# Linear attention followed by a gated long convolution on one core: another order of the same 1477 steps

## The chip, the cores and the metric

The kernel runs on one core of a Trainium2 chip. A core has five engines that run side by side, each with a queue of its own that it works off strictly in order: TensorE (PE, matrix products, with weight loads shown apart as PEld), VectorE (DVE), ScalarE (ACT), GpSimd (POOL) and SyncE (SP), which here only issues DMAs. Engines wait for each other by semaphores. Matrix products are written to PSUM, eight banks of 128 x 2 KB, which DVE and ACT read out to SBUF; POOL works on SBUF alone. The metric is the device time of one execution in microseconds, the median of several runs.

## What is computed

```python
def phi(x):                                   # feature map, 64 -> 2 * 128
    proj = np.einsum('bhsd,df->bhsf', x, w_phi)
    proj = proj - np.max(np.abs(proj), axis=-1, keepdims=True)
    return np.concatenate([np.exp(proj), np.exp(-proj)], axis=-1)
q_p, k_p = (phi(q), phi(k))                   # 8 batches, 8 heads, 576 rows
kv = np.einsum('bhsf,bhsd->bhfd', k_p, v)
z = np.sum(k_p, axis=2)
num = np.einsum('bhsf,bhfd->bhsd', q_p, kv)
den = np.einsum('bhsf,bhf->bhs', q_p, z)[..., None] + 1e-06
x = (num / den)                               # -> (8, 576, 512), heads side by side
...
proj = x @ w_proj                             # (512, 1536): x1, x2, x3
X2 = np.fft.rfft(x2, n=S, axis=1)
H = np.fft.rfft(filter_fft, n=S, axis=0)[None, :, :]
x2_conv = np.fft.irfft(X2 * H, n=S, axis=1)
y = x1 * x2_conv * x3
return (y @ w_out).astype(np.float32)
```

The Fourier transforms over 576 rows are done as matrix products with tables of cosines and sines that the kernel makes itself at the start.

## The kernel before

The whole kernel is a list of words, `PLAN`. The last function, `run`, goes through it and calls one method for each word, so that the list fixes the order on every engine, and with it each engine's queue:

```python
for word in PLAN.split():
    name, _, bank = word.partition("@")
    self.bank = int(bank) if bank else None
    f, *args = name.split(",")
    getattr(self, f)(*[int(a) if a.isdigit() else a for a in args])
```

`X1e,DVE,2,0@6` is the method `X1e` with engine DVE, batch 2, block 0 and PSUM bank 6. Words of one batch are mixed with words of the batches before and after it. Where two words stand next to each other on different engines, the list does not say which runs first; only the order among words of the same engine, and the data, do. All words of one batch `b`, in the order of the data:

- `load` (and `loadh`, half a batch) brings q, k or v in on POOL's DMA queue, in rings of two buffers each; `trh` transposes q and k by DMA on SP's queue. For batch 0, `pt` transposes on PE and `pte` copies out of PSUM.
- `Qn`, `Qnt`, `Pk`, `Pkt` (L638, L646, L631): products with `w_phi` in which the rows lie on the partitions. `maxq`, `maxk`, `maxqt`, `maxkt` (DVE, L707) take the largest absolute value. `ex,k`, `exkt` (ACT, L693, L696) take the exponentials of k, `m` and `p` for the two signs.
- `mhi` (ACT), `mlo`, `trm` (PE), `trme`: the maxima of q, transposed. `Pq`, `Pqt` (L665, L671): q's products the other way round, with the maxima subtracted. `ex,q`, `exqt` (ACT): their exponentials.
- `em` (ACT) and `vs` (L749): v times the exponential of k's maxima, with POOL or DVE. `KV` (L764) sums over the rows, `KVe` copies it out.
- `NE`, `NEt` (L778, L787): the numerator and denominator. `rc`, `rct` and `xn`, `xnt` (DVE, L797, L809) divide.
- `trx`, `trxt` (SP, L816, L821) transpose the result by DMA into `xT`, `xTt`; `ptx`, `ptxe` do it on PE for three quarters of batch 0. `f1` (L846) and `f2` (L852) are folds, sums and differences in SBUF, with POOL or DVE.
- `F` (L858, L862): the transform of the folded rows. `Fe` copies it out, `Xl` repeats a few columns of it. `X2` (L897): the product with the middle third of `w_proj`; `Y1` (DVE, L902, L907): times the filter's spectrum; `m3` (L911): a sum in SBUF, with POOL or DVE.
- `X1`, `X3` (L919) and `X1t`, `X3t` (L928): the other two thirds of `w_proj` with `xT`; `X1e`, `X1te` copy, `tm`, `tmt` (DVE, L960, L964) multiply.
- `I` (L972), `Ie` (ACT), `Ip`, `Im` (DVE, L993), `ym` (L1038), or `J` (L1028) and `yj` (DVE, L1032): back from the spectrum, times x1 x3. `yt` moves the last rows of two batches together.
- `O` (L1049): the product with `w_out`; `Oe` copies it into `o`, a ring of four buffers; `st` (L1058) stores a half of it, on SP's queue or at the very end on ACT's.

At the start there are also the tables (`cols_*`, `gi_*`, `ang`, `frac`, `sin`, `gen_*`), the filter (`fl_load`, `ft`, `fa`, `fb`, `rev`, `Ff`, `Ffe`, `H`, `He`, `Hl`), and `wz`, two products of zeros that have no result and keep PE busy. `w_load` brings the weights in. `copy` gives a copy to ACT if the word says ACT, and to DVE otherwise, so `ft,POOL` runs on DVE (L297).

Of the kernel before, what the change touches and what calls it, by code (L numbers as in the profile page):

```python
# [37 lines left out]
pt,k,0,0,1@3 sin,0 maxq,0,0@4 Pk,0,0@0 pte,ACT,k,0,0,1@3 pt,k,0,1,1@6 fa,POOL,1 pt,k,0,1,0@7
maxk,0,0@0 pte,ACT,k,0,1,1@6 Qn,0,2@4 pte,ACT,k,0,1,0@7 pte,DVE,q,0,1,1@2 maxq,0,2@4 Pk,0,1@6
Qn,0,3@2 ft,POOL fa,POOL,0 maxq,0,3@2 ex,k,m,0,0@0 wz,9@4 Qnt,0@4 ex,k,p,0,0@0 maxqt,0@4 Pk,0,2@2  # L40
maxk,0,2@2 ex,k,m,0,1@6 Pk,0,3@4 w_load,proj,1 rev@0 ex,k,p,0,1@6 maxk,0,3@4 mhi,0 ex,k,p,0,2@2
maxk,0,1@6 ex,k,m,0,2@2 one Pkt,0@6 mlo,DVE,0 ex,k,m,0,3@4 trm,0@2 wz,1@3 maxkt,0@6 trh,q,1,0
fb,0@0 trme,ACT,0@2 wz,12@3 em,m,0,0 ex,k,p,0,3@4 vs,POOL,m,0,0 Pq,0,1@2 trh,q,1,1 fb,1@0 em,p,0,0
exkt,m,0@6 Pq,0,2@4 exkt,p,0@6 ex,q,m,0,1@2 wz,25@0 trh,k,1,0 vs,POOL,p,0,0 ex,q,p,0,1@2 Qn,1,0@0
wz,14@6 trh,k,1,1 em,m,0,1 ex,q,p,0,2@4 maxq,1,0@0 Pq,0,3@2 w_load,proj,2 KV,0,0@6 ex,q,m,0,2@4
vs,DVE,m,0,1 em,p,0,1 ex,q,p,0,3@2 Ff,1@4 vs,POOL,p,0,1 KVe,DVE,0,0@6 Pk,1,1@0 ex,q,m,0,3@2
Ffe,DVE,1@4 Qn,1,3@6 ex,k,m,1,1@0 maxq,1,3@6 NE,0,1@4 Ff,0@2 w_load,proj,0 maxk,1,1@0 KV,0,1@6
Ffe,ACT,0@2 load,v,1 rc,0,1@4 ex,k,p,1,1@0 gen_ends,POOL Pq,0,0@2 xn,0,1@4 KVe,DVE,0,1@6 Qnt,1@4
trx,0,1 ex,q,m,0,0@2 Pk,1,0@0 maxqt,1@4 Ff,2@6 load,k,2 ex,q,p,0,0@2 maxk,1,0@0 NE,0,3@4 load,q,2
# [12 lines left out]
KVe,ACT,1,0@6 load,q,3 late Y1,0,2@5 ex,k,p,2,1@2 trm,1@6 vs,POOL,p,1,1 X2,0,0@7 ex,k,m,2,0@0
trme,DVE,1@6 Y1,0,1@4 X2,0,4@5 ex,k,m,2,1@2 Pq,1,1@0 Y1,0,4@5 load,v,3 X2,0,3@4 ex,q,m,1,1@0
Y1,0,0@7 w_load,out Pkt,2@2 ex,q,p,1,1@0 X1,0,1@5 maxkt,2@2 load,k,3 Y1,0,3@4 X3,0,2@7 exkt,m,2@2
m3,POOL,0,0 exkt,p,2@2 Qn,2,1@0 X1e,ACT,0,1@5 tm,0,2@7 Pq,1,0@2 Pq,1,2@4 maxq,2,1@0 ex,q,m,1,0@2
X1t,0@7 X3t,0@6 ex,q,p,1,0@2 m3,DVE,0,1 X3,0,1@0 X1te,DVE,0@7 em,m,2,0 ex,q,p,1,2@4 tmt,0@6
NE,1,0@2 vs,POOL,m,2,0 tm,0,1@0 J,0,0@6 ex,q,m,1,2@4 rc,1,0@2 xn,1,0@2 NE,1,1@0 trx,1,0 yj,0,0@6
# [6 lines left out]
NEt,1@6 maxq,2,3@2 O,0,1@1 trh,k,3,0 f2,POOL,1,0,0 rct,1@6 O,0,2@0 xnt,1,0@6 Oe,ACT,0,1@1 xnt,1,1@6
maxqt,2@4 Pk,2,3@2 trh,k,3,1 Oe,ACT,0,2@0 F,1,2@6 maxk,2,3@2 F,1,3@4 Fe,ACT,1,2@6 F,1,0@0 trh,q,3,0
Fe,ACT,1,3@4 X1,1,3@6 Fe,DVE,1,0@0 ex,k,m,2,3@2 Qn,2,2@4 st,SP,0,1,0 X1e,DVE,1,3@6 em,m,2,1 F,1,1@0
vs,POOL,m,2,1 trxt,1 maxq,2,2@4 X1,1,2@7 Fe,ACT,1,1@0 Qn,3,2@0 st,SP,0,1,1 mhi,2 X2,1,2@4
X1e,ACT,1,2@7 maxq,3,2@0 ex,k,p,2,3@2 load,q,4 X3,1,2@5 Y1,1,2@4 mlo,POOL,2 load,q,5 trm,2@2
X2,1,1@3 trme,ACT,2@2 em,p,2,1 tm,1,2@5 vs,POOL,p,2,1 Pq,2,0@1 Y1,1,1@3 Qn,3,0@4 Pq,2,1@6
ex,q,m,2,0@1 X3,1,3@0 maxq,3,0@4 ex,q,p,2,0@1 load,k,4 X1,1,0@3 ex,q,p,2,1@6 tm,1,3@0 Pq,2,2@4  # L80
ex,q,m,2,1@6 Pkt,3@0 X2,1,3@2 maxkt,3@0 X2,1,0@6 exkt,m,3@0 Y1,1,3@2 exkt,p,3@0 X1,1,1@7
ex,q,m,2,2@4 Y1,1,0@6 NE,2,1@0 X1e,ACT,1,1@7 X3,1,0@2 X1e,ACT,1,0@3 rc,2,1@0 m3,POOL,1,0 xn,2,1@0
ex,q,p,2,2@4 NE,2,0@6 tm,1,0@2 X1t,1@3 rc,2,0@6 Pqt,2@4 xn,2,0@6 X1te,ACT,1@3 Pq,2,3@0 exqt,p,2@4
Xl,DVE,1 Pk,3,1@2 f1,POOL,2,0,1 KV,2,1@6 trh,q,4,1 exqt,m,2@4 maxk,3,1@2 ex,q,p,2,3@0 f1,POOL,2,0,0
X2,1,4@4 st,SP,0,0,0 KVe,ACT,2,1@6 ex,q,m,2,3@0 trx,2,0 NE,2,2@6 m3,POOL,1,1 Y1,1,4@4 X3t,1@5
ex,k,p,3,1@2 rc,2,2@6 NEt,2@0 xn,2,2@6 trx,2,1 X3,1,1@4 ex,k,m,3,1@2 tmt,1@5 rct,2@0 f2,POOL,2,0,0
xnt,2,0@0 NE,2,3@6 trx,2,2 xnt,2,1@0 I,1,0@2 rc,2,3@6 f2,POOL,2,0,1 xn,2,3@6 Ie,1,0@2 I,1,1@0
Im,1,0@2 trx,2,3 Ie,1,1@0 J,1,2@6 tm,1,1@4 f1,POOL,2,1,0 Ip,1,1@0 Im,1,1@0 trxt,2 Pk,3,2@4 Ip,1,0@2
Pk,3,0@0 yj,1,2@6 ex,k,p,3,2@4 ym,POOL,1,0 J,1,3@2 st,SP,0,3,0 maxk,3,0@0 ex,k,m,3,2@4 st,SP,0,3,1
X1,2,0@6 ym,POOL,1,1 st,SP,0,0,1 yj,1,3@2 ex,k,p,3,0@0 X3,2,0@7 trh,k,4,1 maxk,3,2@4 load,v,4  # L90
em,m,3,0 ex,k,m,3,0@0 O,1,0@2 X1e,DVE,2,0@6 trh,q,4,0 em,p,3,0 F,2,0@4 f1,DVE,2,1,1 X1,2,2@6
# [1023 lines left out]
```

## Time and profile before

| | us |
|---|---|
| three runs | 306.68, 306.43, 314.14 |
| median | 306.68 |
| profiled execution, span from the first to the last instruction | 311.6 |
| busy: PE, DVE, ACT, POOL | 281.0, 268.6, 216.3, 203.8 |
| mean granted clock of PE in that span | 0.974 |

The profiled execution's time beyond its span is not shown. In the rows of the profile a group is named by its line in the code, the engine, the operation and the tiles; "idle before" is the time in which that engine stood still just before, with what ended it.

### The profile page before, as it was taken

To read this page: it belongs to the slowest core of one execution; us is meant where nothing else is said; L and a number is where in the kernel's file an instruction comes from. 1 tells how busy PE (TensorE), PEld (TensorE's weight loads), DVE (VectorE), ACT (ScalarE), POOL (GpSimd) and SP (SyncE) were. 2 spreads that over 40 slices of the span, in tenths; PEclk is the share of its full clock that TensorE was granted. 3 is DMA by queue.
4 is the path that set the end of the run, shared out by engine and by line. 5 is a ranking of instruction groups with operands and counts; after the bars stand their busy time and mean duration, and the time that the engine had idled before them with its cause. 6 is when DMAs were issued, how large, how long until landed. Compare 5 with 4: busy or idle time off the path is not lost.

```text
span 311.6 us, 10240 instructions
## 1 busy us (share of the span) xinstructions
PE 281.0 (90%) x4331; PEld 205.3 (66%) x4360; DVE 268.6 (86%) x447; ACT 216.3 (69%) x345; POOL 203.8 (65%) x163
## 2 busy tenths in 40 slices
PE   1968977999999996999899799999999999999992
...
GB/s 162 235 203 159 136 202 193 105 190 133 91 164 204 94 110 170 116 160 107 114 198 82 131 160 153 172 175 160 84 117 4 56 93 69 19 110 21 1 115 192
DMA packets 72735, 40.20 MB, mean 129 GB/s; under 512 B 53040, under 2 KB 67504, under 8 KB 72688
## 3 DMA queue, kind: packets, MB, share of 16 engines
...
q8 instruction: 34, 0.56, 0.8%
...
## 4 chain that ended last, share of the span: by engine, by line
PE 70%; DVE 12%; DMA 7%; ACT 5%; issue 3%; SPq 1%; POOL 0%; DVEq 0%; POOLq 0%
PE ps L919 16%; PE ps L897 10%; PE ps L1049 8%; PE ps L764 5%; PE ps L972 4%; PE ps L778 4%; DMA xT<-xn 4%; DMA out_dram<-o 3%; PE ps L1028 3%; PE ps L858 3%; PE ps L862 3%; PE ps L928 2%; DVE mq L707 2%; PE ps L665 2%; PE ps L638 2%
## 5 line engine op out<-in xcount | busy, mean ns | idle before, releaser
L919 PE MATMUL ps<-xT,wproj 128*128 128x256 bf16 x512 | 65.8, 275 | 4.3 <-DVE x1s L960 2.3
L919 PEld LDWEIGHTS <-wproj 128*128 128x128 bf16 x512 | 48.6, 98 | 14.5 <-issue 5.1
L707 DVE TENSOR_REDUCE mk<-ps 128x8 f32<-128x1024 f32 (+1 forms) x40 | 44.0, 1110 | 5.9 <-ACT HTo L295 2.2
L707 DVE TENSOR_REDUCE mq<-ps 128x8 f32<-128x1024 f32 (+1 forms) x40 | 44.0, 1110 | 5.5 <-PE ps L638 4.5
L749 POOL TENSOR_TENSOR vm<-vn,vm 128x1152 bf16<-128x1152 bf16 x14 | 30.4, 2178 | 18.2 <-ACT vm L743 18.2
L749 POOL TENSOR_TENSOR vp<-vn,vp 128x1152 bf16<-128x1152 bf16 x16 | 34.8, 2180 | 10.5 <-ACT vp L743 10.3
L911 POOL TENSOR_TENSOR T<-T,T 128x1024 bf16<-128x1024 bf16 x12 | 25.5, 2124 | 21.9 <-DVE T L907 21.8
L693 ACT ACTIVATE Ekp<-ps 128x1024 bf16<-128x1024 f32 x32 | 32.8, 1030 | 6.6 <-DVE mk L707 3.3
L1038 POOL TENSOR_TENSOR yT<-cv,x1s 128x576 bf16<-128x576 f32 x19 | 24.3, 1289 | 18.3 <-DVE x1s L964 12.8
L852 POOL TENSOR_TENSOR xf<-SD 128x512 bf16<-128x512 bf16 x27 | 31.2, 1170 | 6.7 <-DVE SD L846 5.3
L693 ACT ACTIVATE Ekm<-ps 128x1024 bf16<-128x1024 f32 x32 | 32.8, 1033 | 3.6 <-DVE mk L707 2.7
L693 ACT ACTIVATE Eqm<-ps 128x1024 bf16<-128x1024 f32 x32 | 32.9, 1034 | 3.1 <-PE ps L671 2.9
L1049 PE MATMUL ps<-wout,yT 128*128 128x512 bf16 x133 | 34.3, 385 | 0.7 <-issue 0.2
L693 ACT ACTIVATE Eqp<-ps 128x1024 bf16<-128x1024 f32 x32 | 32.5, 1031 | 3.4 <-PE ps L671 3.3
L846 POOL TENSOR_TENSOR SD<-xn 128x512 bf16<-128x512 bf16 x23 | 26.5, 1160 | 12.6 <-DVE xn L797 12.6
L897 PE MATMUL ps<-wproj,XF 128*128 128x512 bf16 x117 | 30.3, 380 | 0.7 <-issue 0.2
L295 ACT CAST x1s<-ps 128x512 bf16<-128x512 f32 (+1 forms) x30 | 16.0, 548 | 13.1 <-PE ps L928 8.4
L797 DVE TENSOR_TENSOR xn<-ps,r 128x512 bf16<-128x512 f32 x32 | 22.0, 689 | 1.1
L1049 PEld LDWEIGHTS <-yT 128*128 128x128 bf16 x144 | 13.4, 99 | 14.1 <-issue 0.6
L990 ACT COPY es<-ps 128x288 f32<-128x288 f32 x21 | 8.5, 404 | 20.3 <-PE ps L972 19.8
L960 DVE TENSOR_TENSOR x1s<-ps,x1s 128x512 bf16<-128x512 f32 x32 | 21.7, 683 | 0.6 <-ACT x1s L295 0.4
L778 PE MATMUL ps<-KVs,Eqp 128*128 128x65 bf16 x256 | 19.6, 192 | 2.2 <-DVE mq L707 0.6
...
## 6 DMA issues: line engine op xcount, KB each, us to landing
...
```

Of the source, the lines that this page charges most:

```text
L693: self.nc.scalar.activation(e, p, AF.Exp, bias=0.0, scale=1.0 if g == "p" else -1.0)
L707: self.nc.vector.tensor_reduce(out=out, in_=src, axis=AX.X, op=ALU.max, apply_absolute_value=True)
L749: self.eng(eng).tensor_tensor(out=t[:, :, :, 0:64], in0=self.at("vn", b)[:, 2 * X:2 * X + 2], in1=t[:, :, :, 64:65].to_broadcast([128, 2, ...
L778: self.mm(self.pb(u, 65 * a, 65 * a + 65), E, KVs[:, u, v, s, :], start=(s == 0), stop=(s == 1))
L797: self.nc.vector.tensor_tensor(out=o, in0=n[:, :, :, 0:64], in1=self.at("r", 4 * b + v).to_broadcast([128, 2, 4, 64]), op=ALU.mult)
L846: self.eng(eng).tensor_tensor(out=o[:, :, 2 * i:2 * i + 2, :], in0=x[:, :, 0:2, :], in1=x[:, :, 2:4, :], op=ALU.subtract if i else ALU.add)
L852: self.eng(eng).tensor_tensor(out=o[:, :, 2 * i:2 * i + 2, :], in0=x[:, :, 0:4:2, :], in1=x[:, :, 1:4:2, :], op=ALU.subtract if i else ALU ...
L897: self.mm(self.pb(0), l, w[:, kt, 512:1024], start=(kt == 0), stop=(kt == 3))
L911: self.eng(eng).tensor_tensor(out=Y, in0=Y, in1=self.at(f"T{2 * e + 1}", b), op=ALU.add)
L919: self.mm(o[:, d], w[:, kt, f0 + 128 * m:f0 + 128 * m + 128], y[:, 1, ::-1, ::-1] if d else y[:, 0], start=(kt == 0), stop=(kt == 3))
L1038: self.eng(eng).tensor_tensor(out=self.at("yT", b)[:, m, 0:SEQ], in0=self.turn_of("cv", (b, m)).rearrange("p x h t -> p (x h t)"), in1=sel ...
L1049: self.mm(self.pb(0), y[:, kt, 128 * c:128 * c + 128], w[:, kt, :], start=(kt == 0), stop=(kt == 3))
```

## The change

Only the list is changed. It has 1477 words before and after, and the same work in them; the order is another on every engine, many words have another PSUM bank, and 88 words have another engine. Counted over the words whose engine differs (before to after, on the engine named):

| word | DVE before | DVE after | the other engine |
|---|---|---|---|
| `f1` | 7 | 5 | POOL 5, 7 |
| `f2` | 4 | 4 | POOL 4, 4 |
| `m3` | 2 | 1 | POOL 1, 2 |
| `vs` | 2 | 1 | POOL 1, 2 |
| `ym` | 2 | 3 | POOL 3, 2 |
| `mlo` | 3 | 0 | POOL 0, 3 |
| `X1e` | 3 | 6 | ACT 6, 3 |
| `Fe` | 4 | 5 | ACT 5, 4 |
| `KVe` | 1 | 3 | ACT 3, 1 |
| `He` | 3 | 4 | ACT 4, 3 |
| `Oe` | 5 | 4 | ACT 4, 5 |
| `pte` | 2 | 1 | ACT 1, 2 |
| `X1te` | 1 | 0 | ACT 0, 1 |
| `ft` | 1 | 0 | ACT 0, 1 |
| `gen_neg` | 0 | 1 | ACT 1, 0 |
| `Ffe`, `Xl`, `trme`, `yt` | 1, 1, 2, 1 | 1, 1, 2, 1 | ACT the same |

The start, before and after:

```diff
-fl_load,2,1 cols_h loadh,q,0,0 zeros fl_load,3,0 gi_part loadh,q,0,1 ident fl_load,0,0 cols_i
-fl_load,1,0 gi_nr loadh,k,0,0 fl_load,1,1 w_load,phi loadh,k,0,1 cols_f load,v,0 fl_loadt ang,2
-gi_fr fl_load,0,1 gz,DVE ang,3 wz,10@0 fl_load,2,0 load,k,1 fl_load,3,1 wz,26@1 load,q,1 frac,3
-pt,q,0,0,0@0 gi_back ang,1 sin,3 pt,q,0,0,1@1 cols_m pte,DVE,q,0,0,0@0 ang,0 wz,13@2
-pte,ACT,q,0,0,1@1 w_phi frac,1 Qn,0,1@0 frac,2 sin,1 wz,20@2 maxq,0,1@0 pt,q,0,1,0@3 pt,q,0,1,1@2
...
+gz,DVE wz,10@0 wz,27@1 gi_part w_load,phi fl_load,0,1 loadh,q,0,0 wz,20@6 loadh,q,0,1 wz,25@3
+wz,9@3 wz,13@3 gi_back zeros gi_nr cols_i fl_load,2,1 cols_f loadh,k,0,0 ang,3 fl_load,2,0 gi_fr
+fl_load,3,0 wz,12@6 wz,14@6 frac,3 ang,0 ident sin,3 ang,2 pt,q,0,0,1@4 fl_load,1,1 loadh,k,0,1
+frac,0 fl_load,3,1 pt,q,0,0,0@6 ang,1 frac,2 wz,26@7 wz,1@3 pte,ACT,q,0,0,1@4 w_phi pt,q,0,1,0@2
+gen_ends,POOL fl_load,0,0 load,q,1 sin,0 pte,ACT,q,0,0,0@6 pt,q,0,1,1@3 Qn,0,1@6 pte,ACT,q,0,1,0@2
+sin,2 Qn,0,2@4 pt,k,0,0,0@2 load,k,1 load,v,0 frac,1 pt,k,0,0,1@1 cols_m pte,ACT,q,0,1,1@3
...
```

Batch 0, around `X3,0,3` and `f2`:

```diff
-vs,POOL,p,1,0 maxk,1,2@2 F,0,1@0 trh,k,2,1 X1e,ACT,0,3@6 X1,0,2@4 Fe,ACT,0,1@0 tm,0,0@5 H,4@6
-em,m,1,1 f2,DVE,0,1,0 ex,k,p,1,2@2 X3,0,3@5 vs,POOL,m,1,0 X1e,DVE,0,2@4 trh,q,2,0 He,ACT,4,0@6
...
+He,DVE,2,0@6 Pk,1,2@2 X1e,ACT,0,0@5 He,DVE,1,0@7 Qn,1,1@0 em,p,1,0 ex,k,p,1,2@2 f2,POOL,0,1,0
+X3,0,0@5 X3,0,3@6 f2,POOL,0,1,1 He,ACT,0,1@4 X1,0,2@4 ex,k,m,1,2@2 He,ACT,1,1@7 maxq,1,1@0
+tm,0,0@5 maxk,1,2@2 vs,POOL,p,1,0 Hl,ACT X1e,DVE,0,2@4 trh,k,2,0 F,0,1@0 X1,0,3@5 Fe,ACT,0,1@0
...
```

The queue of SP from the first store of batch 0 to the last one, the other words left out:

```
before: st,SP,0,1,0 trxt,1 st,SP,0,1,1 trh,q,4,1 st,SP,0,0,0 trx,2,0 trx,2,1 trx,2,2 trx,2,3 trxt,2
        st,SP,0,3,0 st,SP,0,3,1 st,SP,0,0,1 trh,k,4,1 trh,q,4,0 st,SP,0,2,1 ... st,SP,0,2,0
after:  st,SP,0,0,0 trxt,1 st,SP,0,2,0 st,SP,0,0,1 trh,k,3,1 st,SP,0,1,1 st,SP,0,3,1 trx,2,1 trh,k,4,1
        st,SP,0,1,0 st,SP,0,2,1 trx,2,0 trx,2,2 st,SP,0,3,0 trx,2,3
```

The order of `Oe` in batches 0 and 1, which fixes the buffers of `o`, is (0,3) (0,0) (0,1) (0,2) (1,0) (1,2) (1,3) (1,4) (1,1) before, and (0,0) (0,3) (0,1) (0,2) (1,0) (1,3) (1,2) (1,1) (1,4) after.

PE's words between the last `trx` of a batch and the first `X1` on it:

```
batch 2 before: J,1,2 Pk,3,2 Pk,3,0 J,1,3            after: Pk,3,0 J,1,3
batch 3 before: I,2,0 Pk,4,0 J,2,3                   after: X1t,2 X3t,2 I,2,2 Pk,4,0 Pk,4,1 I,2,0 J,2,3
batch 4 before: I,3,2 Pk,5,1 J,3,0                   after: Pk,5,1 J,3,0
batch 5 before: Pk,6,3 Pk,6,1 O,4,3 X2,5,1 X2,5,0 O,4,0 O,4,2 X2,5,3 Pkt,6 Qn,6,0
                                                     after: O,4,0 X1t,5 Qn,6,0 Pkt,6
```

Batch 6's v on POOL, and the end:

```diff
-ex,q,p,4,3@2 rc,4,0@6 load,v,6 xn,4,0@6 O,2,2@5 ex,q,p,4,2@0 m3,POOL,3,0 tm,3,3@4 trx,4,0 NE,4,1@6
...
-Oe,ACT,6,1@5 O,7,2@6 yt,ACT,7 st,SP,6,1,1 O,7,1@7 Oe,ACT,7,2@6 st,SP,6,1,0 O,7,0@5 st,ACT,7,2,0
-st,SP,7,2,1 Oe,DVE,7,1@7 O,7,4@6 st,ACT,7,1,0 st,SP,7,1,1 Oe,DVE,7,0@5 O,7,3@7 st,ACT,7,0,1
-st,SP,7,0,0 Oe,DVE,7,4@6 st,ACT,7,4,0 st,SP,7,4,1 Oe,DVE,7,3@7 st,ACT,7,3,1 st,SP,7,3,0
...
+Y1,5,2@4 load,v,6 X1e,ACT,5,1@1 X1,5,0@7 em,p,6,0 m3,POOL,5,0 Y1,5,4@5 em,m,6,1 Qnt,6@1
+st,SP,4,2,0 maxqt,6@1 Qn,6,1@3 X1,5,3@0 st,SP,3,2,0 vs,POOL,p,6,0 st,SP,3,4,0 maxq,6,1@3
...
+st,SP,6,0,1 st,SP,6,1,1 O,7,0@7 Oe,ACT,7,2@4 st,SP,6,1,0 yt,DVE,7 st,ACT,7,2,0 Oe,DVE,7,1@3
+st,SP,7,2,1 Oe,DVE,7,0@7 st,SP,7,1,1 st,SP,7,0,0 O,7,4@5 O,7,3@2 st,ACT,7,1,0 st,ACT,7,0,1
+Oe,DVE,7,4@5 st,SP,7,4,1 Oe,ACT,7,3@2 st,ACT,7,3,1 st,SP,7,3,0 st,ACT,7,4,0
```

300 lines of the change are left out of this document (150 added, 150 removed).

## Prediction

> **What bounds the kernel now.** I read the page's head first, then the busy time by stretches of 10 us, then the timelines of the engines around the places where TensorE (PE) stood still, and last the chain of waits at the end.
>
> ```profile
> span 311.6 us, 10240 instructions
> PE 281.0 (90%) x4331; PEld 205.3 (66%) x4360; DVE 268.6 (86%) x447; ACT 216.3 (69%) x345; POOL 203.8 (65%) x163
> PE   1968977999999996999899799999999999999992
> PE 70%; DVE 12%; DMA 7%; ACT 5%; issue 3%; SPq 1%; POOL 0%; DVEq 0%; POOLq 0%
> ```
>
> ```profile
> 10.00:20.00 10.00, 6.72 (x90) 4.20 (x91) 9.94 (x17) 9.33 (x14) 5.38 (x3) 0.96 1.20 223
> 50.00:60.00 10.00, 7.67 (x132) 6.16 (x132) 7.56 (x10) 6.10 (x14) 7.44 (x6) 0.83 0.81 138
> 60.00:70.00 10.00, 10.00 (x134) 6.68 (x133) 9.90 (x14) 9.69 (x14) 7.04 (x7) 1.00 1.16 179
> 120.00:130.00 10.00, 8.53 (x66) 5.22 (x68) 7.94 (x11) 4.13 (x9) 5.41 (x4) 0.83 0.63 129
> ```
>
> After each stretch stand the busy times of PE, its weight loads, DVE, ACT and POOL, then the granted clock, the DMA share and GB/s. The start is bound by DVE (9.94 of 10 us) with ACT close behind (9.33). From 60 us on PE is the bound, and a gap in PE is lost time. PE was busy 281.0 of 311.6 us, so 30.6 us are idle, and part of that is the wait for the first data and for the last store: a new order of the same work has that much to win, not more. The clock is the second item: in the two stretches with 0.83 it took 10 x 0.17 = 1.7 us each.
>
> **The frame.** The three timed runs are 306.68, 306.43 and 314.14. The span alone, 311.6, is longer than two of them, so the profiled execution is of the kind of the longest run (then some 2.5 us lie around the span), 7.5 above the median. I make the sum of terms against this execution, and carry to the median only those that a run at 306.7 must hold too.
>
> **Gap 1, batch 0, at 51 us.**
>
> ```profile
> 49.18 2.38 DVE L852 TENSOR_TENSOR xf<-SD 128x512 bf16<-128x512 bf16 x1
> 52.62 0.67 DVE L960 TENSOR_TENSOR x1s<-ps,x1s 128x512 bf16<-128x512 f32 x1
> 49.13 2.15 POOL L749 TENSOR_TENSOR vp<-vn,vp 128x1152 bf16<-128x1152 bf16 x1 [1.65 <-ACT vp L743]
> 53.34 1.87 PE L919 MATMUL ps<-xT,wproj 128*128 128x256 bf16 x8 [2.27 <-DVE x1s L960]
> ```
>
> ```profile
> L852 DVE TENSOR_TENSOR xf<-SD x5: 415/425/2376, 49.2 to 272.8; 128x512 bf16<-128x512 bf16 x5
> L846 DVE TENSOR_TENSOR SD<-xn x9: 411/419/1484, 74.7 to 276.1; 128x512 bf16<-128x512 bf16 x9
> L846 POOL TENSOR_TENSOR SD<-xn 128x512 bf16<-128x512 bf16 x23 | 26.5, 1160 | 12.6 <-DVE xn L797 12.6
> ```
>
> `X3,0,3@5` waits for bank 5, which `tm,0,0@5` (L960) empties. Ahead of `tm` on DVE stands the fold `f2,DVE,0,1,1`: it takes 0.425 us as a rule and here took 2.376, beside a product `vs` on POOL that began 0.05 us before it and lasts 2.15. So PE lost 2.27 us. In the new list `X3,0,3` uses bank 6, which `He,DVE,2,0` sets free much earlier, `tm,0,0` stands one place further ahead on DVE, and both `f2` of this half go to POOL. The term is **-2.3**, between 0 (DVE is full here, so something else may come late) and -2.3. The folds now cost POOL two more and spare it one (`f1,0,0,1` goes to DVE): at 1.16 us each, +1.2 us, less than the 1.65 us that POOL idled before `vs`. Without that cover `vs` of batch 1 would be late by it.
>
> The Trainium skill's page "SBUF — State Buffer", section "SBUF: two separate sides", says that a DVE instruction with two SBUF inputs and a GpSimd instruction that reads SBUF exclude each other for a whole instruction. The trace agrees: 2376 against 425.
>
> **Gap 2, batches 1 and 2, at 119 us.**
>
> ```profile
> 112.05 1.87 SPq L1058 DMA_DIRECT2D out_dram<-o  x3
> 113.32 7.04 DMA out_dram<-o
> 120.46 0.69 DVE L297 COPY o<-ps 128x512 f32<-128x512 f32 x1 [2.99 <-DMA out_dram<-o]
> 121.20 0.28 PE L858 MATMUL ps<-Dt,xnt 128*128 128x288 bf16 x1 [2.38 <-DVE o L297]
> DMA to landing us min/median/max: 2.2/2.8/7.4
> ```
>
> The output ring `o` has four buffers, so `Oe,DVE,1,2` waits until the store of `o` for chunk (0,0) has landed. That store, `st,SP,0,0,1`, stood on SP's queue behind the transposes of batch 2 (`trx,2,*`, `trxt,2`), was issued at 112.6 and took 7.04. DVE waited 2.99, PE 2.38. In the new list all but one of batch 0's eight stores stand ahead of `trx,2,2`; the last, `st,SP,0,3,0`, is followed by `trx,2,3`, and its reader `Oe,ACT,1,3` comes twelve PE words later. Term **-2.4**, between 0 and -2.4.
>
> **The clock in gaps 1 and 2.** In this execution each gap is followed by 1.7 us of lost clock. In the profiled execution that is -3.4 if the gaps go; I take none of it to the median, since its faster runs can have been spared it. The Trainium skill, "TensorE: Matmul & The Clock Gate", section "Part 1: The HAM clock gate", has the clock fall only after an idle window of about 3.4 us. Here gaps of 2.27 and 2.38 us sufficed, so the measurement decides; by the page the clock's 3.4 would not hang on these gaps, and the sum against the profiled span would be -5.0 in place of -8.4.
>
> **The start.**
>
> ```profile
> 17.35 1.20 DVE L297 CAST f<-flt 64x512 bf16<-64x512 f32 x1
> 9.52 0.48 DVE L297 COPY qT<-ps 128x640 bf16<-128x640 bf16 x1
> 15.89 0.41 DVE L297 COPY qT<-ps 128x512 bf16<-128x512 bf16 x1
> 24.08 0.19 DVE L731 TENSOR_TENSOR mh<-mq,mh 128x36 bf16<-128x36 f32 x1
> 2.59 0.23 DVE L345 TENSOR_SCALAR ident<-idx 128x128 bf16<-128x128 f32 x1 [1.42 <-POOL idx L321]
> 13.59 0.68 ACT L1010 ACTIVATE inv<-inv 128x576 bf16<-128x576 bf16 x1
> L295 ACT CAST x1s<-ps 128x512 bf16<-128x512 f32 (+1 forms) x30 | 16.0, 548 | 13.1 <-PE ps L928 8.4 <-PE ps L919 3.2 <-POOL yT L1038 1.3
> ```
>
> DVE loses the cast of the filter's last rows (1.20), two copies of `qT` (0.48, 0.41) and `mlo` (0.19), and takes one copy of `kT` (at 0.41): -1.9 us. The idle 1.42 before `ident` can go too, as `ident` now stands behind the angles. ACT takes the cast (at 0.55) and a copy net (about 0.5) and loses `gen_neg` (0.68): +0.4, on an engine that is nearly as full. So the bounds are +0.4 (ACT decides) and -3.3 (DVE alone decides); nearest to the fuller engine I take **-1.7**. The 20 dummy products `wz` nearly all move ahead of the first data and cost nothing there, while PE has no other work. The loads of q and k for batch 1 now stand ahead of `load,v,0` on POOL's queue; v is first read by `vs` at 26 us, so nothing is lost unless it lands more than a few us later than k and q did.
>
> **Transposes into X1.**
>
> ```profile
> PE ps L919 <- DMA xT<-xn: 1.9, 2, 1.1
> DMA to landing us min/median/max: 2.4/2.7/8.7
> 180.04 1.23 PE ps L1028 x10
> ```
>
> PE waited twice for a transposed `xT`, 1.9 us in all. In batch 3 the old list had `I`, `Pk`, `J` between the last `trx` and the first product `X1` on it, and PE waited there 1.1; the new list has `X1t`, `X3t`, two `I`, two `Pk` and `J`: **-1.1**. But in batch 2 one `Pk` and one `J` (1.23) remain of two and two, in batch 4 the `I` goes and `Pk` and `J` stay, and in batch 5 `trx,5,2` is followed after one `O` and three small steps by `X1,5,1`, where ten words of PE stood, and it has `trh,k,7,1` and `trh,q,7,1` before it on SP. Against 2.7 from issue to landing, and with little more than one `J` (1.23) of PE work in between, each can wait 0 to 1.5 us. I take 1.0 for each, nearest to the 1.1 of batch 3: **+3.0**, bounds 0 and 4.5.
>
> **Engine choices in the middle.**
>
> ```profile
> L749 POOL TENSOR_TENSOR vm<-vn,vm 128x1152 bf16<-128x1152 bf16 x14 | 30.4, 2178 | 18.2 <-ACT vm L743 18.2
> L911 POOL TENSOR_TENSOR T<-T,T 128x1024 bf16<-128x1024 bf16 x12 | 25.5, 2124 | 21.9 <-DVE T L907 21.8
> L1038 POOL TENSOR_TENSOR yT<-cv,x1s 128x576 bf16<-128x576 f32 x19 | 24.3, 1289 | 18.3 <-DVE x1s L964 12.8 <-DVE cv L993 5.4
> DMA to landing us min/median/max: 6.0/7.5/11.6
> 220.00:230.00 10.00, 9.93 (x83) 5.74 (x80) 9.89 (x11) 7.02 (x11) 2.12 (x1) 1.00 0.56 117
> ```
>
> POOL gets one `vs` (2.18), two `f1` (1.16 each), one `m3` (2.12) and three `mlo`, and gives one `ym` back (1.29): about +6 us of 203.8, with 18.2 + 21.9 + 18.3 us of idle time on just these three lines to hide it. DVE and ACT exchange copies; some of each kind go each way, and DVE's sum stays within about 1 us, ACT's falls by 3. One load moves close to its reader: `load,v,6` now stands two instructions ahead of the first `vs` of batch 6 on POOL, with an `m3` (2.12) between, against 7.5 us from issue to landing (the first of the two rows; the second is the stretch in which it happens). POOL can then wait 7.5 - 2.1 = 5.4 us, with two more `m3`, `ym` and `vs` queued behind it, and `KV,6` behind those. But POOL is busy there for only 2.1 of 10 us, so the load can start that much earlier. I cost all of this part at **0**, bounds 0 and +5.4: POOL has idle time to hide it. If that cover is gone, a late `vs` delays `KV`, and a late fold delays `F`.
>
> **The end.**
>
> ```profile
> 303.50 2.79 DMA out_dram<-o
> 306.50 0.69 DVE o L297
> ```
>
> The last products keep their order. `Oe,7,3` still waits for the stores of (7,2), whose 2.79 us stay. The copy `yt`, which stood before `Oe,ACT,7,2` on ACT, goes to DVE, and `Oe,7,3` from DVE to ACT. Term **-0.5**, bounds 0.7 (one copy) either way.
>
> **The sum.** -2.3 - 2.4 - 1.7 - 1.1 + 3.0 + 0 - 0.5 = -5.0. With the clock's -3.4 that is -8.4 on the profiled span, 303.2. On the median: 306.7 - 5.0 = **301.7**.
>
> **The rivals.**
> *The gain is given back (no change).* PE's gaps close, but the start stays bound by ACT (+0.4 in place of -1.7), and the three transposes wait at their upper bound (4.5 in place of 3.0): 301.7 + 2.1 + 1.5 = 305.3. For it: ACT's 9.33 and the shorter leads. Against it: only 2 of 8 batches waited before.
>
> *Folds locked out by POOL (slower).* DVE's folds and products that read SBUF alone number 22 before and 19 after, while POOL works 6 us longer beside them. The rows price one that meets POOL: 2.376 - 0.425 = 1.95 at most, 1.484 - 0.419 = 1.07 for the other line. In the old order the extra was rare (medians 425 and 419). If all 19 pay the 1.07, that is 20 us on an engine that has 43 us of idle time but is 9.90 of 10 busy beside PE in the fullest stretches. If 12 us of it reach PE: 301.7 + 12 = 313.7. It passes the old time from 5 us reaching PE, which is five such meetings at bad places. For it: it made gap 1. Against it: the medians show that most folds run free.
>
> *The order does not do what it says at the start and PE gains more (faster by over 2%).* If the start yields its -3.3 and the new transposes wait nothing: 301.7 - 1.6 - 3.0 = 297.1.
>
> **How the numbers follow.** My forecast has 0.50 (301.7, its own range 299 to 304.5); the gain given back 0.25 (305.3); more gain 0.15 (297.1); locked-out folds 0.10 (313.7). The range takes the forecast, the first rival and most of the third: 297 to 309, its upper end being the first rival's 305.3 with 3.7 of the 5.4 that a late `load,v,6` can cost. Within 2% (about what a measurement of this kernel can tell from no change) means 300.5 to 312.8. Faster by over 2%: 0.15 and 0.4 of the forecast's 0.50, so 0.35. Slower by over 2%: 0.07 of the locked-out folds. The rest, 0.58, is within 2%.
>
> **What would show it.** Right: in the changed profile PE has no gap of 2 us between 45 and 60 us nor one that ends on a copy into `o` around 110 to 125 us, and the stretch clock stays at 1.00 after 60 us; the maxima of batch 0 end about 2 us earlier. Wrong: PE's waits for `xT` sum to over 4 us; L852 or L846 on DVE show medians above 1 us; POOL's `vs` ends last before `KV`; or PE's idle time after 60 us is what it was.

## The result and the profile after

The new list is slower. Against the old list, run beside it, the ratio of the times is 1.081 (95% interval 1.068 to 1.094), some 25 us more. The forecast was 301.7 with a range of 297 to 309; the profiled execution of the new list took 332.87, with a span of 331.1. All ratios are to the old list, run beside the kernel on the same chip; executions that were some per cent longer at a lower granted clock are left out of them, but the old list's profiled one, with a span of 311.6 against its short runs of 306.43 and 306.68, is of that kind.

The page of the new list: span, PE's busy time in 40 equal slices, the granted clock in the same slices, and the shares of the chain of work that ended last.

```profile
span 331.1 us, 10270 instructions
PE   7584249859999799999699999899999799899993
PEclk9858558987999999999999999999999999999998
PE 63%; DMA 14%; DVE 11%; ACT 4%; issue 3%; SPq 2%; POOL 1%; ACTq 0%; DVEq 0%
```

DMA has 14% of the chain, where it had 7%, and PE's slices fall to 4, 2 and 4 between 25 and 50 us and to 5 at 70 us. The same stretches by the busy time of PE, its weight loads, DVE, ACT and POOL, with clock, DMA share and GB/s:

```profile
20.00:30.00 10.00, 5.76 (x45) 2.65 (x45) 8.26 (x14) 9.93 (x17) 7.32 (x6) 0.77 1.32 142
30.00:40.00 10.00, 3.50 (x94) 2.59 (x94) 3.14 (x3) 1.86 (x3) 4.91 (x5) 0.57 1.28 153
40.00:50.00 10.00, 4.28 (x96) 3.72 (x98) 2.89 (x6) 2.33 (x3) 0.00 (x0) 0.50 1.22 195
70.00:80.00 10.00, 5.62 (x31) 2.29 (x25) 9.02 (x6) 4.53 (x6) 5.17 (x4) 0.66 1.19 203
```

From 30 to 50 us the four computing engines stand still most of the time; only the DMA engines are full. What PE waited for, from its list of waits (us in total, times, the longest):

```profile
PE ps L641 <- DMA qT<-qn: 9.6, 2, 5.9
PE ps L634 <- DMA kT<-kn: 6.0, 1, 6.0
PE ps L900 <- DVE XL L300: 4.2, 1, 4.2
PE ps L922 <- DMA xT<-xn: 3.6, 1, 3.6
PE ps L649 <- DMA kT<-kn: 2.0, 1, 2.0
PE ps L781 <- DVE mq L710: 1.8, 1, 1.8
PE ps L781 <- DVE KVs L300: 1.5, 1, 1.5
```

(Lines of the new list stand 3 higher than those of the old.) Two groups: 9.6 + 6.0 + 3.6 + 2.0 = 21.2 us for transposes by DMA, and 4.2 + 1.8 + 1.5 = 7.5 us for DVE. In the old list the like were 1.9 for transposes and 2.3 + 2.4 for the two gaps of the prediction, which are gone. That is 28.7 - 6.6 = 22.1 more, against 331.1 - 311.6 = 19.5 in the spans, or about 26 against the old list's short runs (306.6, less the 1.8 that lie around the span of the new list, is 304.8). The two sums need not agree: PE's first wait, 6.9 in the old list, is 1.2 in the new one, and what the clock of 0.50 to 0.77 in these stretches cost is not taken apart.

**The transposes.** The old list issues the four transposes of batch 1 on SP's queue like this (two in a row each), and loads q and k of batch 2 and a third of `w_proj` on POOL's queue afterwards:

```profile
22.68 3.29 SPq L602 DMA_TRANSPOSE qT<-qn  x2
26.07 2.83 SPq L602 DMA_TRANSPOSE kT<-kn  x2
```

```profile
34.08 0.80 POOL L580 DMA_DIRECT2D wproj<-in_moe_w_proj_dram  x1
37.00 0.78 POOL L590 DMA_DIRECT2D kn<-in_k_dram  x1
37.77 0.75 POOL L590 DMA_DIRECT2D qn<-in_q_dram  x1
```

The new list has these three loads before the second transpose was through:

```profile
17.01 1.93 SPq L605 DMA_TRANSPOSE qT<-qn  x1
20.89 5.49 SPq L605 DMA_TRANSPOSE kT<-kn  x1
26.43 7.82 SPq L605 DMA_TRANSPOSE qT<-qn  x1
34.30 8.05 SPq L605 DMA_TRANSPOSE kT<-kn  x1
```

```profile
22.55 0.78 POOL L593 DMA_DIRECT2D kn<-in_k_dram  x1 [0.31 <-issue]
23.33 0.75 POOL L593 DMA_DIRECT2D qn<-in_q_dram  x1
24.06 0.76 POOL L583 DMA_DIRECT2D wproj<-in_moe_w_proj_dram  x1
```

From issue to landing `qT` took, in the old list and then in the new one:

```profile
DMA to landing us min/median/max: 3.4/3.7/4.0
```

```profile
DMA to landing us min/median/max: 13.3/16.3/19.3
```

The DMA queues in stretches of 2 us show why. q1 is SP's queue with the transposes, q0 POOL's with the loads; packets, MB, share of the 16 engines. First the old list from 27 to 29 us, then the new one from 40 to 42 us:

```profile
q1 hardware_dynamic: 1629, 0.40, 104.8%
```

```profile
q0 software_dynamic: 314, 0.31, 91.6%
q1 hardware_dynamic: 312, 0.08, 29.6%
```

Alone, transposes go at 1629 / 2 = 815 packets per us. Beside loads the two queues move as many packets each: 312 against 314, and nearly equal numbers in every stretch from 30 to 46 us. A transpose then gets 156 packets per us, a fifth. Between 28 and 30 us the transposes got only 181 in 2 us, beside 59 of the loads; why both were so slow there is not shown. The Trainium skill's page "DMA: Bandwidth & Descriptors", section "Queues, rings and completion order", says that each DMA engine goes round the queues that have work, one packet at a time. The equal numbers agree with it; that the packets of this view are the page's packets no run shows.

**DVE locked out.** Between 69 and 75 us, DVE's row and then POOL's rows:

```profile
69.52 5.09 DVE L300 COPY XL<-XF 128x512 bf16<-128x512 bf16 x1
```

```profile
69.43 0.75 POOL L593 DMA_DIRECT2D qn<-in_q_dram  x1
70.19 2.17 POOL L752 TENSOR_TENSOR vm<-vn,vm 128x1152 bf16<-128x1152 bf16 x1
72.30 2.16 POOL L752 TENSOR_TENSOR vp<-vn,vp 128x1152 bf16<-128x1152 bf16 x1
```

The copy `Xl` of batch 0 began while POOL issued a load and ended when the second `vs` behind that load ended (74.61 against 74.46). The three copies of this kind on DVE, and two other groups, with the shortest, the middle and the longest in ns:

```profile
L300 DVE COPY XL<-XF x3: 282/284/5089, 69.5 to 278.5; 128x512 bf16<-128x512 bf16 x3
L1041 DVE TENSOR_TENSOR yT<-cv,x1s x3: 758/1235/3435, 256.3 to 316.4; 128x576 bf16<-128x576 f32 x3
L914 DVE TENSOR_TENSOR T<-T,T x3: 680/735/2551, 185.8 to 308.6; 128x1024 bf16<-128x1024 bf16 x3
```

The second and third row are `ym` (3.44 in place of 0.76, at 256 us) and `m3` (2.55 in place of 0.7, at 286 us), each beside products on POOL, and each just ahead of one of the two last waits of the list. `ym` ended behind the last of three POOL instructions in a row. `m3` got in ahead of the last one: POOL's next product began at 287.54, before `m3` on DVE ended at 288.13, and took 2.57 in place of 2.1.

### The profile page after: what moved, and what is told of

It is laid out like the page before. It is cut to its first block, busy times and chain, and to the rows that moved or that the text cites. A ratio compares the mean times of both kernels' runs of the same rounds, so it can differ in the third digit from the quotient of the medians.

```text
span 331.1 us, 10270 instructions
## 1 busy us (share of the span) xinstructions
PE 283.8 (86%) x4333; PEld 207.6 (63%) x4360; DVE 277.0 (84%) x446; ACT 214.1 (65%) x340; POOL 210.0 (63%) x169
## 4 chain that ended last, share of the span: by engine, by line
PE 63%; DMA 14%; DVE 11%; ACT 4%; issue 3%; SPq 2%; POOL 1%; ACTq 0%; DVEq 0%
PE ps L922 13%; PE ps L900 10%; PE ps L1052 7%; DMA qT<-qn 6%; PE ps L767 5%; PE ps L781 4%; PE ps L975 4%; PE ps L1031 3%; DMA kn<-in_k_dram 3%; PE ps L931 2%; DMA kT<-kn 2%; PE ps L861 2%; PE ps L641 2%; PE ps L865 2%; DMA xT<-xn 2%
## 5 line engine op out<-in xcount | busy, mean ns | idle before, releaser
L922 PE MATMUL ps<-xT,wproj 128*128 128x256 bf16 x512 | 64.9, 273 | 3.6 <-DMA xT<-xn 3.6
L922 PEld LDWEIGHTS <-wproj 128*128 128x128 bf16 x512 | 48.0, 98 | 14.3 <-issue 3.9
L710 DVE TENSOR_REDUCE mk<-ps 128x8 f32<-128x1024 f32 (+1 forms) x40 | 44.2, 1111 | 14.3 <-PE ps L634 10.8
L849 POOL TENSOR_TENSOR SD<-xn 128x512 bf16<-128x512 bf16 x25 | 28.8, 1164 | 33.3 <-DVE xn L800 33.3
L914 POOL TENSOR_TENSOR T<-T,T 128x1024 bf16<-128x1024 bf16 x13 | 28.3, 2179 | 25.0 <-DVE T L910 25.0
L752 POOL TENSOR_TENSOR vm<-vn,vm 128x1152 bf16<-128x1152 bf16 x16 | 35.5, 2223 | 2.1 <-ACT vm L746 2.0
L752 POOL TENSOR_TENSOR vp<-vn,vp 128x1152 bf16<-128x1152 bf16 x15 | 32.3, 2155 | 4.1 <-ACT vp L746 4.1
L1041 POOL TENSOR_TENSOR yT<-cv,x1s 128x576 bf16<-128x576 f32 x18 | 23.0, 1288 | 14.9 <-DVE cv L996 14.9
L900 PE MATMUL ps<-wproj,XF 128*128 128x512 bf16 x117 | 31.3, 394 | 0.6
L298 ACT CAST x1s<-ps 128x512 bf16<-128x512 f32 (+1 forms) x28 | 14.8, 540 | 14.5 <-PE ps L922 6.5
L910 DVE TENSOR_TENSOR T<-ps,HTo 128x1024 bf16<-128x1024 f32 x16 | 19.4, 1218 | 3.3 <-PE ps L900 2.3
L910 DVE TENSOR_TENSOR T<-ps,HTe 128x1024 bf16<-128x1024 f32 x16 | 19.3, 1218 | 2.9 <-PE ps L900 2.8
```

The source lines that it names most:

```text
L710: self.nc.vector.tensor_reduce(out=out, in_=src, axis=AX.X, op=ALU.max, apply_absolute_value=True)
L752: self.eng(eng).tensor_tensor(out=t[:, :, :, 0:64], in0=self.at("vn", b)[:, 2 * X:2 * X + 2], in1=t[:, :, :, 64:65].to_broadcast([128, 2, ...
L849: self.eng(eng).tensor_tensor(out=o[:, :, 2 * i:2 * i + 2, :], in0=x[:, :, 0:2, :], in1=x[:, :, 2:4, :], op=ALU.subtract if i else ALU.add)
L900: self.mm(self.pb(0), l, w[:, kt, 512:1024], start=(kt == 0), stop=(kt == 3))
L910: v.tensor_tensor(out=self.at(f"T{c}", b), in0=p, in1=h, op=ALU.mult)
L914: self.eng(eng).tensor_tensor(out=Y, in0=Y, in1=self.at(f"T{2 * e + 1}", b), op=ALU.add)
```

## The experiments

Theory A: the three loads that moved ahead of the transposes of batch 1 cost most of the loss. Theory B: the loads of batch 1 themselves are late, behind `gen_ends`. Theory C: the dummy products are spent too early. Theory D: DVE is locked out by POOL. A name that begins with a is made from the new list, one with b from the old.

**a_loads_back**

```diff
-cols_h load,k,2 em,p,0,0 ... load,q,2 fb,0@0 w_load,proj,0 vs,DVE,p,0,0
+cols_h em,p,0,0 ... fb,0@0 vs,DVE,p,0,0
-vs,POOL,p,0,1 Pq,0,3@2
+vs,POOL,p,0,1 load,k,2 load,q,2 w_load,proj,0 Pq,0,3@2
```

> Changed list, with load,k,2, load,q,2 and w_load,proj,0 moved back on POOL's queue, behind vs,POOL,p,0,1 (they are then issued at about 33 us, not 22.6 to 24.1). Theory A (the four transposes of batch 1 share the DMA engines with these loads, 1.6 MB, and so take 13 to 21 us each): the second to fourth transposes land in about 4 us, TensorE's waits for qT and kT (3.7 + 6.0 + 5.9 us) fall to under 5 in all, and the time falls by 10 to 15 us, to 318 to 322. Theory B (the loads of batch 1 go out too late, behind gen_ends): no more than 2 us, 330 to 333. Theory C (the loss comes from dummy products spent too early, hence a low clock): the waits stay and the time stays within 2 us.

Measured: ratio 1.028 (1.017 to 1.040), so 5.3 of the 8.1 per cent are gone. The four transposes land after 13.6, 10.5, 8.0 and 5.0 us: the loads still ahead of them run out. The moved loads now meet the transposes of batch 2.

**b_loads_early**

```diff
-w_load,proj,1 ... w_load,proj,0 load,v,1 gen_ends,POOL ... load,k,2 ... load,q,2
+w_load,proj,1 load,k,2 load,q,2 w_load,proj,0 ... load,v,1 gen_ends,POOL
```

> Old list, with load,k,2, load,q,2 and w_load,proj,0 moved forward on POOL's queue, right behind w_load,proj,1 (issued at about 19 to 21 us, not 34 to 38), nothing else changed. Theory A: the transposes of batch 1, issued at 22.7 to 27.5 us, take 10 us or more in place of 3.4 to 4.0, and the time rises by 8 to 15 us, to 315 to 322. Theories B and C: no change, 305 to 308, since the loads of batch 1 and the dummy products stand where they stood.

Measured: ratio 1.055 (1.041 to 1.068). PE's waits, and `qT` to landing:

```profile
PE ps L638 <- DMA qT<-qn: 7.3, 1, 7.3
PE ps L631 <- DMA kT<-kn: 7.0, 1, 7.0
```

```profile
DMA to landing us min/median/max: 13.4/15.0/16.5
```

The old list has the loss as soon as these three words are moved, with nothing else of the change in it. Theory A holds both ways.

**a_gen_ends_back**

```diff
-gen_ends,POOL fl_load,0,0 load,q,1 ... load,k,1 load,v,0
+fl_load,0,0 load,q,1 ... load,k,1 load,v,0 gen_ends,POOL
```

> Changed list, with gen_ends,POOL moved behind load,v,0, so that the loads of q and k of batch 1 and v of batch 0 go out about 2 us sooner. Theory B (late loads): the first transposes start 2 us sooner and the time falls by 3 us or more, below 329. Theory A: the transposes still meet the loads of batch 2, and the time stays within 2 us of 332.

Measured: 1.076 (1.066 to 1.086), the same as the new list within the interval. The loads of batch 1 went out up to 3 us sooner (q at 6.19 in place of 9.15), but the first transpose did not (17.29, against 17.01), and PE's waits for `qT` and `kT` stayed (10.2 and 5.3 us). Theory B falls.

**a_xl_act**

```diff
-Xl,DVE,0
+Xl,ACT,0
```

> Changed list, with Xl of batch 0 on ACT instead of DVE. Theory D (the copy, one SBUF input, took 5.09 us in place of 0.28 because DVE waited until two products vs on POOL were through): the copy takes 0.6 us on ACT, TensorE's wait of 4.2 us before X2 of batch 0 goes, and the time falls by 3 to 5 us, to 327 to 329. Rival (the copy ended late because something else held DVE): DVE's next instruction is late instead, and the time stays within 1.5 us of 332.

Measured: 1.060 (1.050 to 1.070), and the wait of 4.2 us is no longer in the list. DVE's next instruction began at 69.51, with POOL's two products where they were, and PE's first product on `XL` at 70.48 in place of 74.67. So nothing else held DVE, and the wait was on the path. The 2.1 per cent are 6.5 us, more than the wait, and the intervals overlap; the spans differ by 3.7 (327.4 against 331.1).

**a_v_loads**

```diff
-m3,POOL,0,1 ... st,SP,0,1,1 load,v,3 ... load,v,4 f2,POOL,3,0,0 ... f2,POOL,3,0,1
+m3,POOL,0,1 load,v,3 ... st,SP,0,1,1 ... f2,POOL,3,0,0 ... f2,POOL,3,0,1 load,v,4
```

> Changed list, with load,v,3 moved forward behind m3,POOL,0,1 (about 86 us, not 106.4) and load,v,4 back behind f2,POOL,3,0,1 (about 166 us, not 155.7), nothing else. Theory A, at two other places (transposes issued 1.6 and 4.2 us behind a load of 590 KB took 6.65 and 6.16 us): both land in 2.5 to 4 us, the waits of 2.0 for kT and 3.6 for xT go, and the time falls by 3 to 6 us, to 326 to 329. Rival (these transposes are late because SP issued them late, behind stores and other transposes): the waits stay within 1 us of what they are, time 331 to 333.

Measured: 1.065 (1.057 to 1.073). The waits of 2.0 and 3.6 us are gone. `xT` to landing from 95 to 170 us, in the new list and then here:

```profile
DMA to landing us min/median/max: 2.4/3.7/7.7
```

```profile
DMA to landing us min/median/max: 2.4/3.4/4.2
```

So theory A holds at two more places.

**a_start_mended**

```diff
+load,v,0 load,q,1 ... load,k,1 gen_ends,POOL
+vs,POOL,m,0,1 w_load,proj,0 w_load,proj,2 vs,POOL,p,0,1 w_load,proj,1 load,v,1 load,k,2 load,q,2
+load,k,3 w_load,out ... Xl,ACT,0
```

> Changed list with the whole start of the load queue put right: load,v,0 before load,q,1 and load,k,1, gen_ends,POOL behind them; behind vs,POOL,m,0,0 the order w_load,proj,0, w_load,proj,2 (one vs further on), w_load,proj,1, load,v,1, load,k,2, load,q,2, so that each pair of tensors to be transposed is the last in the queue; w_load,out behind load,k,3; and Xl of batch 0 on ACT. Theory A: now the transposes of batch 1 and of batch 2 meet an almost empty load queue and land in 3 to 6 us, the waits for qT, kT and wproj fall under 2 us in all, and the time falls 6 to 12 us below the 320.8 of the first mending: 309 to 314. Rival (only the loads of batch 2 beside the transposes of batch 1 matter, the rest of the loss at the start lies in the order of DVE or ACT): 315 to 321.

Measured: 1.052 (1.041 to 1.063), a miss. The transposes of batch 1 landed in 3.5 us as expected. But k and q of batch 2 were now the last of six loads, their transposes went out at 52 to 61 us beside `load,v,2`, and PE waited 8.6 us for `kT`. The harm was moved by one batch; how much of it is the late landing of these loads and how much the meeting with `load,v,2` is not taken apart.

**b_store_first** and **b_fold_pool**

```diff
-st,SP,0,0,0 trx,2,0 trx,2,1 trx,2,2 trx,2,3 trxt,2 st,SP,0,3,0 st,SP,0,3,1 st,SP,0,0,1
+st,SP,0,0,0 st,SP,0,0,1 trx,2,0 trx,2,1 trx,2,2 trx,2,3 trxt,2 st,SP,0,3,0 st,SP,0,3,1
```

```diff
-f2,DVE,0,1,1
+f2,POOL,0,1,1
```

> Old list, with st,SP,0,0,1 moved forward on SP's queue, from behind trx(2) to right behind st,SP,0,0,0. If the term of gap 2 was right, TensorE's wait of 2.4 us for the copy into o at 119 us goes, nothing takes its place, and the time falls by 2.4 us (ratio 0.992). Rival: the transposes of batch 2 are now later and PE waits for them instead, ratio 1.000.

> Old list, with the one fold f2 of batch 0 that met a product vs on POOL (2.38 us in place of 0.43) moved from DVE to POOL. If the term of gap 1 was right, TensorE's wait of 2.3 us before X3,0,3 goes and the time falls by 2 to 2.3 us (ratio 0.993). Rival: the vs behind the fold on POOL is late by 1.2 us and delays KV of batch 1, ratio 0.998 to 1.002.

Measured: 0.995 (0.990 to 1.0004) and 0.996 (0.990 to 1.002). Each wait went, in each case alone too little to be told from no change.

**b_both**, the two together.

> Old list with both single edits of b_store_first and b_fold_pool. If they add up, ratio 0.991 to 0.985 (303.8 to 302); if each only hands its wait on to the next instruction, 0.995 to 1.000.

Measured: 0.983 (0.975 to 0.992). The stretches behind the two gaps, which had 7.67 and 8.53 of PE at a clock of 0.83:

```profile
50.00:60.00 10.00, 9.99 (x157) 7.12 (x154) 8.85 (x13) 9.54 (x19) 9.97 (x7) 1.00 0.79 139
120.00:130.00 10.00, 10.00 (x177) 6.54 (x174) 8.85 (x11) 5.61 (x11) 6.82 (x4) 1.00 0.95 169
```

The size is known to about half a per cent: the means of the four shortest runs and of the eleven shortest of the old list beside them, 305.5 and 309.0, give 0.989. The clock, however, does not follow from the gaps. In b_store_first the first gap is still there, again 2.27 us long, and the clock stayed at 1.00:

```profile
50.00:60.00 10.00, 7.67 (x147) 6.46 (x147) 9.01 (x11) 7.52 (x17) 8.43 (x6) 1.00 0.85 138
```

In b_fold_pool the second gap is still there (1.91 us), and the clock behind it is 1.00 as well.

**a_all_mended**: the start as in a_start_mended, but `w_load,proj,1` left in its place, and

```diff
+vs,POOL,p,0,1 load,v,1 load,k,2 load,q,2
+vs,POOL,p,1,1 load,k,4 load,q,3 load,v,2
+KVe,DVE,7,0@0 m3,DVE,6,0 ... xn,6,0@2 ym,DVE,5,2
```

with `load,v,3` and `load,v,4` as in a_v_loads.

> Changed list with every place mended that the profiles showed so far. Loads: load,v,0 before load,q,1 and load,k,1, gen_ends,POOL behind them; w_load,proj,0 and w_load,proj,2 behind vs,POOL,m,0,1; load,v,1, load,k,2, load,q,2 behind vs,POOL,p,0,1; load,k,4, load,q,3, load,v,2 behind vs,POOL,p,1,1; w_load,out behind load,k,3; load,v,3 and load,v,4 as in a_v_loads. DVE: Xl of batch 0 on ACT, ym,DVE,5,2 behind xn,6,0 and m3,DVE,6,0 behind KVe,DVE,7,0. If the loss of 25.5 us is the sum of transposes that met loads (about 14 at the start and 4 later) and of DVE instructions locked out by POOL (4.2 + 1.8 + 1.5), the time is 306 to 309, about that of the kernel before. If the forecast of 301.7 was right but for these, 301 to 304. If something else in the list costs time, above 311.

Measured: 1.006 (1.001 to 1.010). Of 8.1 per cent 7.5 go when the loads that met transposes and the DVE instructions that met POOL are moved. The four longest waits of PE that are left behind 33 us:

```profile
PE ps L634 <- DMA kT<-kn: 2.1, 1, 2.1
PE ps L1052 <- POOL yT L1041: 1.7, 1, 1.7
PE ps L767 <- POOL vp L752: 1.3, 1, 1.3
PE ps L1052 <- DMA wout<-in_moe_w_out_dram: 0.9, 1, 0.9
```

**a_all_wz**

```diff
-wz,20@6 ... wz,25@3 wz,9@3 wz,13@3
+Qn,0,2@4 wz,20@7 ... Pk,0,0@0 wz,25@7 ... Pk,0,2@2 wz,9@7 ... maxk,0,1@6 wz,13@7
```

> The list of a_all_mended, with four of the twenty dummy products' words (wz,20, wz,25, wz,9, wz,13) moved from before the first data to places among the products of batch 0, on bank 7, near to where the old list has such words. If the dummies cost nothing where the changed list has them, the time stays within 1 us of a_all_mended. If the low clock from 10 to 30 us (0.55 to 0.8, against 0.96 and 0.70 before) is on the path, the granted clock there rises and the time falls by 1 to 2 us.

Measured: 1.008 (1.003 to 1.013), no gain. The granted clock from 10 to 30 us rose from 0.64 and 0.85 to 0.95 and 1.00, and it did not matter: PE is not the bound there. As a cause of the 25 us theory C falls; a gain of 1 us could not be told from none.

**b_k_early** and **b_kq_early**: the dose, one load and two loads of the three of b_loads_early.

```diff
+w_load,proj,1 load,k,2
```

```diff
+w_load,proj,1 load,k,2 load,q,2
```

> Old list, with load,k,2 alone moved forward behind w_load,proj,1 (a third of the bytes of b_loads_early). In the profiles the two DMA queues alternate one packet of a load with one of a transpose while both have work (about 150 of each per us; a transpose alone goes at about 800). By that, the 540 packets of this load hold the transposes up by 540/150 - 540/800 = 2.9 us: TensorE's waits for qT and kT of batch 1 sum to 1 to 4 us, and the time rises by 1 to 4 us (ratio 1.003 to 1.013). Rival, the slowdown comes with any load in flight, whatever its size: waits of over 8 us, ratio above 1.03.

> Old list, with load,k,2 and load,q,2 moved forward behind w_load,proj,1 (two thirds of the bytes of b_loads_early; b_k_early has one third). If the slowdown follows the load's packets, the transposes of batch 1 end between those of the two runs, TensorE's waits for qT and kT before 45 us lie between 0.9 and 14.3, at 4 to 9 us, and the ratio between 1.027 and 1.055. If any load in flight does the full harm, or only the last load (w_load,proj,0) did it, they are as in one of the two runs.

Measured: 1.027 (1.019 to 1.034) and 1.023 (1.017 to 1.028), with PE's waits for the transposes of batch 1 at 0.9 and 4.8 us, and 14.3 with all three. `qT` to landing, with one load and with two (3.7 with none, 15.0 with three in the middle):

```profile
DMA to landing us min/median/max: 5.6/6.2/6.9
```

```profile
DMA to landing us min/median/max: 10.5/10.8/11.2
```

In the trace the harm grows with the loads, so the rival of full harm by any load falls. The ratio of b_k_early, above the expected 1.013 and no lower than with two loads, cannot speak against that. Its five runs spread from 311.06 to 320.97. The three longest average 319.1, and over the 310.8 of the old list beside them that is the 1.027; the two shortest, 311.06 (the one in the trace) and 314.68, give 1.007, which is inside the expected 1.003 to 1.013.

**b_start_engines**

```diff
-pte,DVE,q,0,0,0@0 gen_neg,ACT pte,ACT,k,0,0,1@3 pte,DVE,q,0,1,1@2 ft,POOL mlo,DVE,0
+pte,ACT,q,0,0,0@0 gen_neg,DVE pte,DVE,k,0,0,1@3 pte,ACT,q,0,1,1@2 ft,ACT mlo,POOL,0
```

> Old list in its old order, with the engines of the start as the changed list has them: both copies of qT and the cast of the filter's last rows on ACT, one copy of kT and gen_neg on DVE, mlo of batch 0 on POOL. If the term of the start was right, the maxima of batch 0 end about 1.5 us sooner and the time falls by 1.7 us (ratio 0.9945). If ACT decides at the start, KV of batch 0 starts no sooner, and the ratio is 0.999 to 1.004.

Measured: 0.985 (0.976 to 0.995), on two runs. The instruction behind the last maximum of batch 0 on DVE, in the old list and then here:

```profile
25.63 2.34 DVE L502 TENSOR_TENSOR fe<-turn,ps 128x1024 bf16<-128x1024 f32 x2
```

```profile
24.84 2.34 DVE L502 TENSOR_TENSOR fe<-turn,ps 128x1024 bf16<-128x1024 f32 x2
```

It comes 0.79 us sooner, and `KV` of batch 0 with it (29.63 in place of 30.43): a gain, about half the size that was forecast. The ratio, 4.6 us, is more than this accounts for; on two runs it is not taken as a size.

**a_mended_2**

```diff
-vs,POOL,p,1,1 load,k,4 load,q,3 load,v,2 ... load,k,3 w_load,out ... m3,POOL,0,1 load,v,3
+vs,POOL,p,1,1 load,v,2 load,k,4 w_load,out ... load,k,3 ... m3,POOL,0,1 load,q,3 ... vs,POOL,m,2,0 load,v,3
```

> a_all_mended with the loads around 58 to 67 us spread by when they are read: load,v,2, load,k,4, w_load,out behind vs,POOL,p,1,1, load,q,3 behind m3,POOL,0,1 and load,v,3 behind vs,POOL,m,2,0. In a_all_mended five loads stood in one row there, transposes beside them took 13 to 15 us, and TensorE waited 0.9 for wout and 1.7 for yT. If these were what is left, the ratio to before falls from 1.0056 to 0.995 or less. If not, it stays at 1.003 to 1.008.

Measured: 1.013 (1.008 to 1.018), a miss in the wrong direction. Three loads go out beside the four `trx` of batch 1 (at 68.39, 73.39 and 74.19), which took 14.62 us to issue; but in a_all_mended these had taken 12.92 already, and PE waits no more than 0.4 us for an `xT`.

```profile
70.94 14.62 SPq L819 DMA_TRANSPOSE xT<-xn  x4
```

PE's new wait is another one, for nothing that the profile shows:

```profile
81.66 0.23 PE L781 MATMUL ps<-KVs,Eqp 128*128 128x65 bf16 x1 [4.61 <-issue]
```

From 76.8 to 81.7 us the queue that brings instructions moved one packet, beside 542 of loads and 322 of transposes. That PE's code was late behind them is possible and not shown.

**b_three**: b_both and b_start_engines in one.

> Old list in its old order with the three parts of the forecast that the new order was to bring: the store of b_store_first, the fold of b_fold_pool and the engines of b_start_engines. Alone they gave ratios of 0.995, 0.996 and 0.985, the first two together 0.983. If the parts add up, the ratio is 0.967 to 0.98 (about 300 to 303) and the forecast's sizes hold where no load meets a transpose. If the start's gain is swallowed by a later wait, 0.98 to 0.99.

Measured: 0.988 (0.982 to 0.995). The parts do not add up (0.967 to 0.98 was expected for that); the ratio lies in the interval of b_both, in the range that was expected if a later wait swallows the start's gain. Which wait that would be is not shown. Like b_both it is faster than the old list by its interval.

## Why the prediction was wrong

**The step that failed is in the part on the start**, which put the moved loads at nothing: "The loads of q and k for batch 1 now stand ahead of `load,v,0` on POOL's queue; v is first read by `vs` at 26 us, so nothing is lost unless it lands more than a few us later than k and q did." It asked only when the data of a moved load lands and is read. It did not list the loads of batch 2 and of `w_proj`, which had moved forward by 10 to 14 us on POOL's queue, and did not ask what they would share the DMA engines with: the transposes on SP's queue. Those took 13 to 21 us from issue to landing in place of 3.4 to 4.0. b_loads_early shows this step alone to be worth 1.055, and a_loads_back takes 5.3 of the 8.1 per cent away.

**Transposes into X1** (-1.1 and +3.0). The place that was forecast to gain, batch 3, lost: 3.6 us, behind `load,v,4`. The three places with a shorter lead, forecast at 1.0 each, show no wait for a transpose in the list of PE's waits. The step took the median landing (2.7) and gave the longest of the same row (8.7) no term, so it did not ask what makes a landing long. In batch 3 not the work of PE in between but the load in flight decided; a_v_loads shows it.

**Folds locked out by POOL**, the rival for a slower kernel, did occur, at 0.10. It cost 7.5 us of PE's time. Two of its terms were off: it counted folds and products with two inputs, and the costliest case is a copy with one (`Xl`); and it took 1.95 us as the most that a meeting can cost, while 5.09 - 0.28 = 4.81 and 3.44 - 0.76 = 2.68 were paid (the third, 2.55 - 0.68 = 1.87, is below it). The Trainium skill, "SBUF — State Buffer", section "SBUF: two separate sides", names DVE instructions in a two-port performance mode beside those with two inputs, and the prediction used only the second half. That this copy runs in such a mode no run here shows; that it ends with POOL's row, and that nothing else held DVE (a_xl_act), the traces show.

**Gaps 1 and 2** (-2.3 and -2.4) were right. Neither wait is in the new list, and b_both, with both undone in the old list, gives 0.983 (0.975 to 0.992), where 4.7 of 306.7 is 0.985. The long store of gap 2 was issued at 113.3, third in its row, not at 112.6; that changes no term.

**The clock** (-3.4 on the profiled span): that gaps of 2.27 and 2.38 us "sufficed" does not hold as a rule. The same gap of 2.27 us was followed by a clock of 0.83 in the old list's profile and by 1.00 in b_store_first, so the gap alone does not decide; what does stays open.

**The start's term** (-1.7): right in sign, half in size (0.79 by the trace of b_start_engines; in the new list the last maximum of batch 0 ends at 24.68, against 25.71). That ACT decides instead was wrong in b_start_engines. In the new list none of it reached PE: `KV` of batch 0 began at 30.58, against 30.43.

**The dummy products** cost nothing where they are, as forecast (a_all_wz). **The end** (-0.5) was not tried by itself; from the last `yj` to the end of the span the old list's profile has 10.8 us and the new one's 10.7. **`load,v,6`**, with its bound of +5.4, shows no wait of PE. All three terms in one, gaps and start, come to 1.2 per cent in b_three (0.5 to 1.8), where the forecast had 6.4 of 306.7, 2.1 per cent.

What stays open is the last 0.6 per cent and why it is not a gain: the waits of a_all_mended sum to 6.0 us in the four rows shown, about what lies between it and the forecast, but the one attempt to remove some of them (a_mended_2) brought a longer one.
